# Moving small attention steps behind what they read in an attention-then-SwiGLU kernel

## The chip, the cores and the metric

One core of a Trainium2 chip runs the whole program. The engines are TensorE (PE in the profile; its weight loads are PEld), VectorE (DVE), ScalarE (ACT), GpSimd (POOL) and SyncE (SP), which issues the transfers. Each takes its instructions in program order. The metric is the device time of one execution, in microseconds (us); lower is better.

## The reference

For each of B = 4 batches, x has N = 12416 rows of C = 128 numbers, and 32 inducing points attend to x; then x attends to the result h; then every row goes through a gated unit of width 1536.

```python
def mab(q, kv):
    s = scale * (q @ kv.transpose(0, 2, 1))
    a = np.exp(s - s.max(-1, keepdims=True))
    a /= a.sum(-1, keepdims=True) + 1e-09
    return a @ kv
h = mab(I, x)             # first softmax, over the 12416 rows
y = mab(x, h)             # second softmax, over the 32 points
g = y @ w_gate            # 128 -> 1536
out = (g / (1 + np.exp(-g)) * (y @ w_val)) @ w_out    # 1536 -> 128
```

## The kernel before

The rows of a batch are cut into 25 column tiles of 480 or 512 rows, and the 1536 hidden columns into NT = 12 tiles of 128. One *slot* is one hidden tile of one column tile, so a batch has 25 x 12 = 300 slots. The second attention's product with h is folded into the up-projection weights, so a slot multiplies the softmax weights (the `stack` tile: high and low halves of the second softmax, transposed) by prepared weights.

In a slot TensorE does two up-projections (gate and value, line 900 in batches 1 to 3, lines 859 and 860 in batch 0), ScalarE applies silu (`gates`, line 910), VectorE multiplies (`values`, line 917), ScalarE rounds the product to its high half (`splits`, line 925), GpSimd forms the low half h_lo (line 927), and some slots later TensorE does three down-projections (`back`, lines 944 to 946) into an output tile, whose twelve slots end with an eviction by VectorE (line 954) and a store issued by SP (line 958). Batches 1 to 3 do two slots at a time, a *pair*, named by its first slot; there gate and value each fill one of three double PSUM banks. Some pairs hand half of their high and low halves to VectorE (`owned`). Finished tiles wait in a list `pend` before `back` takes them; the list is held at 8 tiles, and grows to 14 before a *burst*, a slot with a long exponential, in which TensorE lives off the list.

While batch b runs its slots, the attention of batch b+1 is threaded in. `plan` and `post` write a list of (slot, step); at each slot the loop runs all steps whose slot has come, the current batch's first. A step that needs an output bank carries `acc`, and is held back, with all behind it in its list, while the oldest tile of `pend` is the last or one of the first two (three for `hacc`) of its output group.

The steps that matter here:

- `s1_visit`, `s2_visit`: TensorE forms the scores of several chunks of x (line 366; there are 7 chunks), and VectorE takes each out of its bank (s1: line 401; s2 transposes, line 592). The first chunk of a visit takes a bank of the two-bank output pool; so does a visit of a single chunk.
- `size_a` to `size_d`: powers of two that scale h; `size_c` and `size_d` are four tiny ScalarE instructions (`grow`, line 527).
- `s2_max`, `s2_sub` (line 604, GpSimd), then `exp2` (line 607, ScalarE): the second exponential over the whole batch. Its slot is e2, set by the entry E2 of PA (batch 0's loop) and PB (the loops of batches 1 and 2). Then `proj_rounds` and `proj_spread` make the next batch's weights.
- `post`, for each of the 7 column chunks q of the second softmax: `sum2` (VectorE, lines 297 and 298), `rec2` (reciprocal on VectorE, line 614, and for batches 1 to 3 a scaling on ScalarE, line 616), `norm2` (GpSimd, line 620), `aT` (VectorE transpose, line 624), `a_hi` (VectorE, line 627), `a_lo` (GpSimd, line 640), and `spread` (line 657), four transfers per column tile that build its `stack`; tile 0 takes sixteen. aT, a_hi and a_lo have one buffer each; `stack` has three. Chunk 0 is tile 0, each later chunk four tiles.

The steps of chunks 0 and 1 fall at the end of the batch before (bases 266 and 278), the others at bases 26, 74, 122, 170 and 218.

Of the kernel before, what the change touches and what calls it, by code (L numbers as in the profile page):

```python
# [38 lines left out]
NT = DFF // P  # L39
# [14 lines left out]
NST = 3  # L54
# [50 lines left out]
    62: "sb:84:97:1",  # L105
}

PA = dict(LX=(51, 5), S1=(61, 7), MX=7, E1=15, LN=(27, 4), HA=(3, 3, 3), HB=(9, 6), HC=(8, 4), HD=5, H2=6, E2=5, PR=(0, 3), PQ=2)
PB = dict(LX=(0, 9), S1=(25, 7), MX=6, E1=9, LN=(28, 4), HA=(3, 3, 3), HB=(11, 3), HC=(8, 4), HD=6, H2=5, E2=5, PR=(0, 3), PQ=1)


@with_exitstack
def induced_set_attention_then_swiglu(ctx: ExitStack, tc: tile.TileContext, xt, xn, ind, wgv, wo, out):
# [17 lines left out]
    def two():  # L131
        del spare[:]
        return ps_two.tile([P, 2 * 512], F32, name="gw")
# [123 lines left out]
    class Piece:  # L257
# [23 lines left out]
        def add(self):  # L281
            nc.gpsimd.tensor_add(out=self.w.bitcast(I32), in0=self.t.bitcast(I32), in1=self.lw.bitcast(I32))
# [22 lines left out]
    def attention(b, one, xn0=None, xt0=None):  # L305

        st = Batch()
# [304 lines left out]

        def rec2(q):
            nc.vector.reciprocal(out=st.sm[q][:, :FC[q]], in_=st.sm[q][:, :FC[q]])
            if st.half:
                nc.scalar.activation(out=st.sm[q][:, :FC[q]], in_=st.sm[q][:, :FC[q]], func=AF.Copy, scale=2.0 ** TOP)

# [92 lines left out]
    def post(st, q, eng, base, ready=0):  # L710

        f = st.f
        steps = [(0, lambda: f["sum2"](q)), (1, lambda: f["rec2"](q)), (2, lambda: f["norm2"](q, eng)),
                 (5, lambda: f["aT"](q)), (7, lambda: f["a_hi"](q)), (9, lambda: f["a_lo"](q, eng))]
        tiles = [u for u, (p, j) in enumerate(COLS) if p == q]
        return [(base + d, g) for d, g in steps] + [
            (max(base + 12, ready + NT * (u - NST + 1) + 3), lambda u=u: f["spread"](u)) for u in tiles]

    def plan(st, p):

        f, s = st.f, []

        def add(slot, step, *args):
            def go():
                f[step](*args)


            go.acc = (NT - 1, 0, 1) + (2,) * (step == "hacc") if step in ("s1", "max_b", "hacc", "h_c", "s2", "size_b", "s1_visit", "s2_visit") else ()
            s.append((slot, go))

        def blocks(q):
            return CH0[q], CH0[q] + CH[q]

        last = p["S1"][0] + p["S1"][1] * (NCH - 1)
        v1 = last - 3 * p["S1"][1]
        for q in range(NCH):
            add(p["LX"][0] + p["LX"][1] * q if q < NXT else v1 + 1 + 3 * (q - NXT), "load_xt", q)
            if not st.wide:
                add(v1 if q < NXT else last, "s1", q, q not in (0, NXT))
        if st.wide:  # L740
            add(v1, "s1_visit", 0, 1, 2), add(v1, "s1_visit", 3)
            add(last, "s1_visit", 4, 5, 6)
        mb = last + p["MX"]
        add(last + 2, "max_a"), add(mb, "max_b")
        e1 = mb + p["E1"]
        for q in range(NXN):
            add(e1 - p["LN"][0] + p["LN"][1] * q, "load_xn", q)
            add(e1, "exp1_part", q)
            add(e1, "eT", q)
            add(e1 + p["HA"][q], "hacc", q, (0, NXN - 1))  # L750
        add(e1, "exp1_part", NXN, NCH - 1)
        for q in range(NXN, NCH):
            k = NXN + (q - NXN | 1)
            at = e1 + p["HB"][0] + p["HB"][1] * (k - NXN)
            add(max(at - p["HC"][0] - k + q, e1 + 1 + (p["HB"][0] + p["HB"][1] if q == NCH - 1 else p["HA"][0])), "load_xn", q)
            add(at - p["HC"][1] + 1 - k + q, "eT", q)
            add(at, "hacc", q, (k - 1, k))
        add(at, "h_a")
        add(at + 2, "h_b")
        hn = at + p["HD"]  # L760
        add(hn, "h_c")
        for i, step in enumerate(("size_a", "size_b", "size_c", "size_d")):
            add(hn + (2, 8, 12, 16)[i], step)
        for i, q in enumerate(S2O):
            k = i % NXT
            at = hn + 4 + p["H2"] * (NXT - 1) if i < NXT else hn + p["H2"] * (NCH - 1)
            if not st.wide:
                add(at, "s2", *blocks(q), i not in (0, NXT))
            elif i in (0, NXT):
                add(at, "s2_visit", *S2O[i:i + 3])  # L770
            elif i == 3:
                add(at, "s2_visit", q)
            if i + NXT < NCH:
                add(at + 1, "load_xt", S2O[i + NXT])
            d = 2 if i < NXT else 1
            add(at + 1 + d * k, "s2_max", *blocks(q))
            add(at + 3 + (d + 1) * k, "s2_sub", *blocks(q))
        e2 = at + 4 + p["E2"]
        add(e2, "exp2")
        st.e1, st.bursts = e1, {e1, e2}  # L780
        add(e2 + p["PR"][0], "proj_rounds")
        for i in range(2):
            for k in range(NG * NG):
                add(e2 + p["PR"][i] + 3 + k * p["PQ"], "proj_spread", i, k // NG, k % NG)
        for q in range(NF):
            first = [u for u, (p, j) in enumerate(COLS) if p == q][0]
            s += post(st, q, nc.gpsimd, SLOTS + NT * (first - NST) + 2, SLOTS)
        return sorted(s, key=lambda x: x[0])
# [5 lines left out]
    with tc.tile_pool(name="xt0", bufs=NCH - NXT) as xt0, tc.tile_pool(name="xn0", bufs=NCH - NXN) as xn0:  # L794
        cur = attention(0, one, xn0, xt0)
        f = cur.f
# [16 lines left out]
        def run(token):  # L813
# [17 lines left out]
            at=f["aT"], ah=lambda q, e=0: f["a_hi"](q, (f["same"], nc.scalar.copy)[e]),  # L831
# [53 lines left out]
    def twin(x, u):  # L885

        return x.rearrange("p (k w) -> p k w", k=2)[:, :, :u.n]

    def fronts(st, b, c, t):
        us = []  # L890
        g, v = two(), two()
        for k in range(2):
            u = Tile()
            us.append(u)
            u.q, u.j = COLS[c]
            u.b, u.t, u.st, u.whole = b, t + k, st, False
            u.n = WF if u.q == 0 else 32 * FC[u.q]
        for k, x in enumerate((g, v)):
            for u in us:
                nc.tensor.matmul(out=x[:, 512 * (u.t - t):][:, :u.n], lhsT=st.w[:, wcol(k, u.t)], rhs=st.stack[c][:, :u.n], start=True, stop=True)  # L900
        u.g, u.v, u.us = twin(g, u), twin(v, u), us
        return u
# [70 lines left out]
    pend, wait = [], []  # L973
# [14 lines left out]
    for b in range(B):  # L988
        nxt = attention(b + 1, (one, oneb)[(b + 1) % 2]) if b + 1 < B else None
        if nxt is not None:  # L990
            nxt.steps = plan(nxt, PA if b == 0 else PB)
            if b == 0:
                cur.steps.append((nxt.e1, lambda: run(f"e2:52:{NTB}")))
                for q in range(2, NF):
                    base = NT * (1 + NG * (q - 1) - NST) + 2
                    base = max(base, E0 + 4) if q < 4 else max(base, nxt.e1 + 1)
# [14 lines left out]
        for slot2 in range(NT if b == 0 else 0, SLOTS, size):  # L1011
            c, t = slot2 // NT, slot2 % NT
            slots = range(slot2, slot2 + size)
            burst = any(x in bursts for x in slots)
            if size == 1:
                u = front(cur, b, c, t)
                u.us = [u]
                u.last = False
                u.cast_dve = burst or t in CAST
                gate(u)  # L1020
                value(u)
            else:
                u = fronts(cur, b, c, t)
                u.last = b == B - 1 and slot2 == SLOTS - 2
                u.cast_dve = burst
                u.own = u.last or owned(slot2, burst)
                gates(u)
                values(u)
            if wait:
                parts(wait[0])  # L1030
                pend += wait.pop(0).us
            wait.append(u)
            if burst:
                parts(u)
                pend += wait.pop(0).us
            def steps(slot):
                for a in (cur, nxt):
                    while a is not None and a.steps and a.steps[0][0] <= slot:

                        if pend and pend[0].t in getattr(a.steps[0][1], "acc", ()):  # L1040
                            break
                        if getattr(a.steps[0][1], "acc", ()):
                            quiet["step"] = slot + 8
                        a.steps.pop(0)[1]()

            for slot in slots:
                if size == 1:
                    steps(slot)
                ahead = min(ahead + size / RAMP, top_) if nxt is not None and slot < last_burst else max(ahead - 1 / RAMP, low_)
                if slot in bursts:  # L1050
                    ahead = low_ - (b == 0)
                while len(pend) + sum(len(x.us) for x in wait) > ahead + (slot != slots[-1]):
                    back(pend.pop(0))
                if size == 2:
                    steps(slot)
# [46 lines left out]
```

## Time and profile before

| | |
|---|---|
| median of 3 runs | 1446.11 us (1444.27 to 1446.88) |
| the profiled execution | 1444.72 us, span 1442.9 us |
| batch 1 / 2 / 3, first up-projection | 410.34 / 760.61 / 1112.81 us |
| granted TensorE clock | 1.00 |
| second exponential, one instruction | 2.80 us |

In the rows of the profile, "out<-in" names the program's tiles, "xN" is a count, and a bracket at the end of a timeline row is the engine's idle time before that instruction with what ended it. A list of waits has the total in us, the number and the longest.

### The profile page before, as it was taken

What the parts mean: (1) busy time and instruction counts of PE and PEld (TensorE: products, weight loads), DVE (VectorE), ACT (ScalarE), POOL (GpSimd) and SP (SyncE); (2) the same over time, 40 slices, a digit from 0 to 9 for tenths busy, and PEclk for the clock granted to TensorE, in tenths of its full rate; (3) what the DMA queues carried; (4) which work ended last, traced back from release to release, by engine and by line L of the source; (5) the groups of instructions that cost most, each with busy time, mean ns of one, the idle gap of its engine ahead of it and who ended that gap; (6) DMA issues with size and microseconds to landing.
All of it is one profiled execution on the core that took longest, in us unless ns stands there. A gap on an engine that the chain in (4) does not pass through costs nothing. (4 is left out here: it accounts for less than half of the span.)

```text
span 1442.9 us, 22347 instructions
## 1 busy us (share of the span) xinstructions
PE 1398.7 (97%) x7462; PEld 770.0 (53%) x7462; DVE 1184.9 (82%) x1704; ACT 1213.6 (84%) x1600; POOL 1186.1 (82%) x783
## 2 busy tenths in 40 slices
PE   9999999999999999999999999999999999999998
PEld 6577778788854444344444444344444444444444
DVE  6889988888888777688888877778888888888887
ACT  5888788799897888788989888788888888888887
POOL 1689768889888888888888888888888888888887
PEclk9999999999999999999999999999999999999999
DMA  9234522311132432110103413211111001010010
GB/s 370 69 100 133 181 74 90 114 46 46 32 102 75 158 123 99 37 50 29 31 25 114 160 65 126 98 35 41 32 32 32 30 28 32 30 34 27 27 32 28
DMA packets 50803, 107.75 MB, mean 75 GB/s; under 512 B 12928, under 2 KB 32896, under 8 KB 50688
## 3 DMA queue, kind: packets, MB, share of 16 engines
q1 hardware_dynamic: 50688, 106.33, 21.9%
q8 instruction: 59, 0.97, 0.3%
q14 instruction: 56, 0.46, 0.1%
HBM read 62.87 MB, written 25.43 MB: 61 GB/s over the span
## 5 line engine op out<-in xcount | busy, mean ns | idle before, releaser
L927 POOL TENSOR_TENSOR h_lo<-h,h_hi 128x1024 f16<-128x1024 f32 (+2 forms) x450 | 821.4, 1840 | 154.2 <-ACT h_hi L925 151.2
L917 DVE SCALAR_TENSOR_TENSOR h<-gw,sc,silu 128x1024 f32<-128x1024 f32 (+2 forms) x450 | 502.1, 1117 | 163.8 <-ACT silu L910 151.6
L910 ACT ACTIVATE silu<-gw,sc 128x1024 f32<-128x1024 f32 (+1 forms) x451 | 489.3, 1086 | 99.0 <-PE gw L900 45.4
L925 ACT CAST h_hi<-h 128x1024 f16<-128x1024 f32 (+3 forms) x446 | 404.3, 907 | 14.0 <-DVE h L917 13.4
L944 PE MATMUL o<-h_hi,work 128*128 128x512 f16 (+1 forms) x900 | 335.8, 373 | 0.3 <-DVE h_lo L927 0.3
L945 PE MATMUL o<-h_hi,work 128*128 128x512 f16 (+1 forms) x900 | 335.8, 373 | 0.0
L946 PE MATMUL o<-h_lo,work 128*128 128x512 f16 (+1 forms) x900 | 335.8, 373 | 0.0
L900 PE MATMUL gw<-stack,work 128*128 128x512 f16 (+1 forms) x1200 | 303.6, 373 | 18.1 <-ACT silu L910 16.5
L883 POOL TENSOR_TENSOR h_lo<-h,h_hi 128x512 fp32r<-128x512 f32 (+1 forms) x216 | 269.5, 1272 | 56.4 <-ACT h_hi L881 35.0
L900 PEld LDWEIGHTS <-work 128*128 128x128 f16 x1200 | 116.4, 98 | 158.1 <-issue 29.5
L865 ACT ACTIVATE silu<-gv 128x512 f32<-128x512 f32 (+1 forms) x300 | 176.6, 590 | 25.8 <-PE gv L859 20.3
L873 DVE TENSOR_TENSOR h<-gv,silu 128x512 f32<-128x512 f32 (+1 forms) x216 | 143.4, 667 | 35.5 <-ACT silu L865 16.5
L900 PE MATMUL gw<-stack,tw 128*128 128x512 f16 (+1 forms) x600 | 152.4, 373 | 10.6 <-ACT silu L910 9.6
L944 PEld LDWEIGHTS <-work 128*128 128x128 f16 x900 | 88.1, 98 | 102.7 <-issue 2.9
L945 PEld LDWEIGHTS <-work 128*128 128x128 f16 x900 | 87.8, 98 | 101.9 <-issue 3.7
L946 PEld LDWEIGHTS <-work 128*128 128x128 f16 x900 | 87.9, 98 | 100.6
L881 ACT CAST h_hi<-h 128x512 fp32r<-128x512 f32 (+1 forms) x190 | 115.4, 607 | 10.2 <-DVE h L873 8.6
L859 PE MATMUL gv<-stack,tw 128*128 128x512 f32 (+1 forms) x300 | 120.2, 401 | 2.9 <-DVE stack L701 1.2
L860 PE MATMUL gv<-stack,tw 128*128 128x512 f32 (+1 forms) x300 | 116.8, 389 | 0.7 <-ACT silu L865 0.4
L944 PE MATMUL o<-h_hi,wo_lo 128*128 128x512 f32 (+1 forms) x288 | 112.6, 391 | 0.0
L946 PE MATMUL o<-h_lo,wo_hi 128*128 128x512 f32 (+1 forms) x288 | 111.3, 387 | 0.1
L945 PE MATMUL o<-h_hi,wo_hi 128*128 128x512 f32 (+1 forms) x288 | 111.0, 385 | 0.0
(217 smaller groups left out, 1373.8 us busy)
## 6 DMA issues: line engine op xcount, KB each, us to landing
xt_sb<-xt SPq DMA_DIRECT2D x32, 896.0 KB, 5.1
xn_sb<-xn SPq DMA_DIRECT2D x18, 896.0 KB, 6.5
out<-ob SPq DMA_DIRECT2D x52, 256.0 KB, 2.0
out<-ob SPq DMA_DIRECT2D x48, 240.0 KB, 2.0
xt_sb<-xt SPq DMA_DIRECT2D x4, 832.0 KB, 4.7
xn_sb<-xn SPq DMA_DIRECT2D x3, 832.0 KB, 4.6
stack<-a_hi SPq DMA_DIRECT2D x72, 32.0 KB, 1.8
stack<-a_lo SPq DMA_DIRECT2D x72, 32.0 KB, 1.8
```

Source lines behind the costliest of these rows:

```text
L859: nc.tensor.matmul(out=u.g[:, :n], lhsT=st.w[:, wcol(0, t)], rhs=rhs, start=True, stop=True)
L865: nc.scalar.activation(out=u.s[:, :u.n], in_=u.g[:, :u.n], func=AF.Silu)
L873: nc.vector.tensor_mul(out=u.h[:, :n], in0=u.v[:, :n], in1=u.s[:, :n])
L883: eng.tensor_sub(out=u.lo[:, :n], in0=u.h[:, :n], in1=u.hi[:, :n].bitcast(F32))
L900: nc.tensor.matmul(out=x[:, 512 * (u.t - t):][:, :u.n], lhsT=st.w[:, wcol(k, u.t)], rhs=st.stack[c][:, :u.n], start=True, stop=True)
L910: nc.scalar.activation(out=f(u.s), in_=f(u.g), func=AF.Silu, scale=u.st.g)
L917: nc.vector.scalar_tensor_tensor(out=h, in0=f(u.v), scalar=u.st.k, in1=f(u.s), op0=ALU.mult, op1=ALU.mult)
L925: (nc.vector.tensor_copy if h is u.x else one_wide if u.cast_dve else nc.scalar.copy)(out=f(u.hi), in_=h)
L927: (nc.vector if h is u.x else nc.gpsimd).tensor_sub(out=f(u.lo), in0=h, in1=f(u.hi))
L944: nc.tensor.matmul(out=o[:, :n], lhsT=w_lo[:, ws], rhs=u.hi[:, :n], start=(t == 0), stop=False)
L945: nc.tensor.matmul(out=o[:, :n], lhsT=w_hi[:, ws], rhs=u.hi[:, :n], start=False, stop=False)
L946: nc.tensor.matmul(out=o[:, :n], lhsT=w_hi[:, ws], rhs=u.lo[:, :n], start=False, stop=(t == NT - 1))
```

## The change

`rec2` is split: the ScalarE scaling becomes a step of its own, `scale2`. For batches 1 to 3 it comes five slots after the reciprocal, and the steps behind it come 5 (norm2), 6 (aT, a_hi, a_lo, and the first spread's own offset) slots later than before. The second exponential moves from E2 = 5 to 8 in batch 0's loop and to 11 in those of batches 1 and 2, and with it the burst and the weights behind it. The single-chunk visits come two slots after the visits of three. `size_c` and `size_d` come 8 and 10 slots later. At the first pair of batch 1, where the PSUM pools change, one finished tile's `back` is issued ahead of the first up-projections.

```diff
-PA = dict(..., E2=5, PR=(0, 3), PQ=2)
-PB = dict(..., E2=5, PR=(0, 3), PQ=1)
+PA = dict(..., E2=8, PR=(0, 3), PQ=2)
+PB = dict(..., E2=11, PR=(0, 3), PQ=1)
...
         def rec2(q):
             nc.vector.reciprocal(out=st.sm[q][:, :FC[q]], in_=st.sm[q][:, :FC[q]])
+
+        def scale2(q):
             if st.half:
                 nc.scalar.activation(out=st.sm[q][:, :FC[q]], in_=st.sm[q][:, :FC[q]], func=AF.Copy, scale=2.0 ** TOP)
...
-        steps = [(0, lambda: f["sum2"](q)), (1, lambda: f["rec2"](q)), (2, lambda: f["norm2"](q, eng)),
-                 (5, lambda: f["aT"](q)), (7, lambda: f["a_hi"](q)), (9, lambda: f["a_lo"](q, eng))]
+        at = (1, 6, 7, 11, 13, 15, 18) if st.half else (1, 2, 2, 5, 7, 9, 12)
+        steps = [(0, lambda: f["sum2"](q)), (at[0], lambda: f["rec2"](q)), (at[1], lambda: f["scale2"](q)), (at[2], lambda: f["norm2"](q, eng)),
+                 (at[3], lambda: f["aT"](q)), (at[4], lambda: f["a_hi"](q)), (at[5], lambda: f["a_lo"](q, eng))]
...
-            (max(base + 12, ready + NT * (u - NST + 1) + 3), lambda u=u: f["spread"](u)) for u in tiles]
+            (max(base + at[6], ready + NT * (u - NST + 1) + 3), lambda u=u: f["spread"](u)) for u in tiles]
...
-            add(v1, "s1_visit", 0, 1, 2), add(v1, "s1_visit", 3)
+            add(v1, "s1_visit", 0, 1, 2), add(v1 + 2, "s1_visit", 3)
...
-            add(hn + (2, 8, 12, 16)[i], step)
+            add(hn + (2, 8, 20, 26)[i], step)
...
             elif i == 3:
-                add(at, "s2_visit", q)
+                add(at + 2, "s2_visit", q)
...
+                if b == 1 and slot2 == 0:
+                    back(pend.pop(0))
                 u = fronts(cur, b, c, t)
```

More of the change, by code (lines that the diff above doesn't have):

```diff
@@ L106 @@
 }
-PA = dict(LX=(51, 5), S1=(61, 7), MX=7, E1=15, LN=(27, 4), HA=(3, 3, 3), HB=(9, 6), HC=(8, 4), HD=5, H2=6, E2=5, PR=(0, 3), PQ=2)
-PB = dict(LX=(0, 9), S1=(25, 7), MX=6, E1=9, LN=(28, 4), HA=(3, 3, 3), HB=(11, 3), HC=(8, 4), HD=6, H2=5, E2=5, PR=(0, 3), PQ=1)
+PA = dict(LX=(51, 5), S1=(61, 7), MX=7, E1=15, LN=(27, 4), HA=(3, 3, 3), HB=(9, 6), HC=(8, 4), HD=5, H2=6, E2=8, PR=(0, 3), PQ=2)
+PB = dict(LX=(0, 9), S1=(25, 7), MX=6, E1=9, LN=(28, 4), HA=(3, 3, 3), HB=(11, 3), HC=(8, 4), HD=6, H2=5, E2=11, PR=(0, 3), PQ=1)
 @with_exitstack
```

## The prediction

> **What bounds the kernel now.** I read the page first, then the list of waits for TensorE, then the same list for the engines that TensorE waits for, then the timeline at single places.
>
> ```profile
> span 1442.9 us, 22347 instructions
> PE 1398.7 (97%) x7462; PEld 770.0 (53%) x7462; DVE 1184.9 (82%) x1704; ACT 1213.6 (84%) x1600; POOL 1186.1 (82%) x783
> ```
>
> TensorE is the bound, so only its stalls are worth anything. The list of waits of TensorE (who waited for whom, total us, times, longest), and the same row in the windows 410 to 438 and 760 to 790 us, where batches 1 and 2 begin; and, from TensorE's timeline, its stall behind the second exponential of batch 1's loop:
>
> ```profile
> PE gw L900 <- ACT silu L910: 26.1, 27, 1.9
> PE o L366 <- DVE s_all L592: 2.1, 2, 1.1
> ```
> ```profile
> PE gw L900 <- ACT silu L910: 1.1, 4, 0.5
> PE gw L900 <- ACT silu L910: 0.9, 2, 0.7
> ```
> ```profile
> 602.59 0.59 PE L900 MATMUL gw<-stack,work 128*128 128x512 f16 x2 [1.94 <-ACT silu L910]
> ```
>
> The up-projections of batches 1 to 3 wait 26.1 us for ScalarE's silu: the silu that frees their PSUM bank is late. What makes ScalarE late is in ScalarE's own list:
>
> ```profile
> ACT sm L616 <- DVE sm L614: 34.3, 19, 2.1
> ...
> ACT s_all L607 <- POOL s_all L604: 6.4, 2, 3.2
> ACT sm L616 <- DVE negmax L419: 3.1, 2, 1.6
> ```
>
> Line 616 is the scaling of the second softmax's reciprocals, issued right behind VectorE's reciprocal of line 614. ScalarE waits there 21 times (19 + 2), two of them in batch 0's loop, 19 in batches 1 to 3; and twice, 3.2 us each, the second exponential (L607) waits for GpSimd's subtractions.
>
> One such place in batch 3 (slots 172 to 176). ScalarE, then VectorE, then TensorE by pairs of slots (each window runs from one pair's first up-projection to the next; length, busy time, matmuls):
>
> ```profile
> 1301.17 0.98 ACT L925 CAST h_hi<-h 128x960 f16<-128x960 f32 x1
> 1304.17 0.21 ACT L616 ACTIVATE sm<-sm 128x15 f32<-128x15 f32 x1 [2.02 <-DVE sm L614]
> 1304.29 1.04 ACT L910 ACTIVATE silu<-gw,sc 128x960 f32<-128x960 f32 x1
> ```
> ```profile
> 1302.99 0.65 DVE L297 TENSOR_REDUCE pairs<-s_all 128x15 f32<-128x480 f32 x1
> 1303.67 0.18 DVE L298 TENSOR_REDUCE sm<-pairs 128x15 f32<-128x30 f32 x1
> 1303.89 0.25 DVE L614 RECIPROCAL sm<-sm 128x15 f32<-128x15 f32 x1
> 1305.43 1.22 DVE L917 SCALAR_TENSOR_TENSOR h<-gw,sc,silu 128x960 f32<-128x960 f32 x1 [1.29 <-ACT silu L910]
> ```
> ```profile
> 1301.58:1303.60 2.02, 2.02 (x11) 1.00 0.00 0
> 1303.60:1307.00 3.40, 2.19 (x11) 1.00 0.00 0
> 1307.00:1309.15 2.15, 2.15 (x11) 1.00 0.00 0
> ```
>
> The reader should see a chain: VectorE is a pair behind, ScalarE stands 2.02 us for a 0.21 us instruction, the silu behind it starts late, and a pair takes 3.40 us in place of 2.02, the next 2.15. The loss is 1.38 + 0.13 = 1.51 us, while TensorE's idle time there is 3.40 - 2.19 = 1.21: 0.30 more. The granted clock is 1.00 in all three, so no part of it is the clock.
>
> The Trainium skill (Perfetto Trace Analysis, Identifying the Most-Contended Engine) warns that matmul busy time says little about headroom, since matmuls are pipelined; the trace agrees by these 0.30 us. By idle time alone the next sum would be 20.2 where start-to-start lengths give 25.9.
>
> **The change, part by part.** The sum is made against the profiled execution, 1444.72 us (span 1442.9); the median of the runs is 1446.11, 1.4 above.
>
> *1. scale2 five slots behind rec2 (b > 0), its followers moved along.* No instruction is added. Of the 26.1 us, 2.0 belong to the batch starts and 3.9 to the two second exponentials (part 3), so 20.2 us in 27 - 6 - 2 = 19 stalls are left, one for each ScalarE wait in batches 1 to 3. With 0.30 more each: 20.2 + 5.7 = 25.9 us. In the new order ScalarE reaches scale2 three pairs, some 6 us, behind VectorE's reciprocal, so the wait goes. What is late next is VectorE, which keeps its work: free at 1304.1, it does pair 172's products by 1305.3 and, for a pair half handed to it, cast and subtraction (about 0.65 each, as the reduction of the same 480 columns), and starts pair 174's products near 1306.6, 3.0 us behind that pair's first matmul. How late they may be:
>
> ```profile
> 1310.16 1.18 DVE L917 SCALAR_TENSOR_TENSOR h<-gw,sc,silu 128x960 f32<-128x960 f32 x1
> ```
> ```profile
> 1311.19 0.37 PE L900 MATMUL gw<-stack,work 128*128 128x480 f16 x1
> ```
>
> Pair 176 (first matmul 1307.00) had its products at 1310.16, 3.15 us behind, and pair 180, which needs that bank, began at 1311.19, 2.04 behind its predecessor: no stall. So 3.0 just fits. I leave 0.1 us per place (bounds 0 and 1.0, the latter if VectorE stays late): 25.9 - 1.9 = 24.0 us.
>
> The followers (norm2 on GpSimd, aT and a_hi on VectorE, a_lo on GpSimd, first spread on SP) come 4 to 6 slots later. For one chunk this puts aT and a_hi behind the first exponential's burst, not ahead of it. VectorE stands idle there once:
>
> ```profile
> 514.89 1.28 DVE L917 SCALAR_TENSOR_TENSOR h<-gw,sc,silu 128x1024 f32<-128x1024 f32 x1 [3.42 <-ACT silu L910]
> ```
>
> aT comes behind these products in program order and misses that gap; the two operations (0.65 us each) delay products by at most one of them. I take 0.3 us in each of two batches (bounds 0 and 0.65): -0.6.
>
> The spreads are SP's. Tile 0's sixteen transfers (slot 279, now 284) fall behind the output store of tile 23, which they preceded; SP takes its queue in order and that store waits for VectorE:
>
> ```profile
> SPq L958 <- DVE ob L954: 592.9, 71, 14.1
> ```
> ```profile
> 734.52 2.41 SPq L657 DMA_DIRECT2D stack<-a_hi  x4
> 737.91 2.41 SPq L657 DMA_DIRECT2D stack<-a_lo  x4
> 740.36 2.49 SPq L657 DMA_DIRECT2D stack<-a_hi  x4
> 742.89 2.49 SPq L657 DMA_DIRECT2D stack<-a_lo  x4
> 746.70 0.34 SPq L958 DMA_DIRECT2D out<-ob  x1
> ```
> ```profile
> 748.31 0.67 DVE L627 TENSOR_REDUCE a_hi<-aT 128x512 f16<-128x512 f32 x1
> ```
> ```profile
> DMA to landing us min/median/max: 1.7/1.8/8.0
> ```
>
> There is one a_hi buffer: the a_hi of chunk 1 (748.31) must wait until the twelfth transfer (last of the second a_hi group) has landed. Before, that was about 742.9 + 1.2 = 744.1, 4 us early. Now the sixteen start at 747.1; the twelfth is issued 11 x 0.62 us later, at 753.9, and lands at 755.7. The a_hi comes six slots later, 748.31 + 6.06 = 754.4: VectorE waits 1.3 us. With its own lateness (up to 0.9) against the 1.1 us it may be late, that stalls TensorE 0 to 1.2 us, and chunk 1's a_lo on GpSimd waits likewise for the sixteenth, with the h_lo of later tiles queued behind it; TensorE has eight tiles in store against that. I take 0.7 at two boundaries and 0.3 at the first, where slots are issued singly: -1.7 (bounds 0 and -6). The Trainium skill (DMA: Bandwidth & Descriptors, Anatomy of one DMA) gives about 2.0 us as the fixed part, for GpSimd's path; by it each landing is 0.2 later than by the row's 1.8 and the sum 0.6 us smaller.
>
> In batch 0's loop both scale waits go as well. TensorE's one idle row near them:
>
> ```profile
> 392.64 0.48 PE L859 MATMUL gv<-stack,tw 128*128 128x480 f32 x1 [1.00 <-DVE h L873]
> ```
>
> VectorE also does other work there, so I take 0.8 (bounds 0 and 1.0).
>
> *2. Fourth chunk of scores two slots on.* In the first softmax no wait of TensorE stands at this chunk, so 0; the code also holds that step back while the oldest stored tile is the last or one of the first two of an output group, so it comes at slot 51. In the second the wait is the row of 2.1 us, twice 1.07:
>
> ```profile
> 567.31 0.91 PE L366 MATMUL o<-xt_sb,hTs 128*32 128x416 f32 x8 [1.07 <-DVE s_all L592]
> ```
>
> Its 0.91 us of matmuls stay, now behind the next pair, when VectorE has emptied the bank: +2.1 (bounds 1.5 and 2.3). That pair also gets scale2 and size_c's three scalings, four ScalarE instructions of about 0.21; the chunk's 0.91 us cover them.
>
> *3. Second exponential six slots on (three in batch 0).* ScalarE and GpSimd in batch 1:
>
> ```profile
> 592.84 1.28 ACT L607 ACT_TABLE_LOAD   x1
> 597.31 2.80 ACT L607 ACTIVATE s_all<-s_all 128x3104 f32<-128x3104 f32 x1 [3.19 <-POOL s_all L604]
> 600.13 1.28 ACT L910 ACT_TABLE_LOAD   x1
> ```
> ```profile
> 596.34 0.94 POOL L604 TENSOR_TENSOR s_all<-s_all,mx2b 128x448 f32<-128x448 f32 x1
> ```
>
> ScalarE does no silu for 8.57 us, 3.19 of it waiting; TensorE's stored work covers all but the 1.94 us shown first. Without the wait 5.4 us are left, under the 6.6 that were covered. GpSimd's last subtraction ends at 597.28, plus about 1 us for the norm2 that now joins its queue; the exponential, ready at 594.1, comes six slots (6.4 us) later, less some 2.5 us that are saved ahead of it (a stall of 1.4 as above, 1.1 at the chunk), at 598.0: 0.3 us of wait at worst. Gain 2 x (1.94 + 0.30) = 4.5, less 0.3: 4.2 (bounds 2.0 and 4.5). If GpSimd's h_lo are late after it, tiles stored fewer: -0.5 (0 to -2). Batch 0's exponential has no wait row: 0.
>
> *4. size_c and size_d later:* ScalarE's list has no wait at their line, so 0. *5. One down-projection ahead of batch 1's first up-projection:* it fills up to 0.65 us of waiting, but that up-projection starts no sooner and the pairs behind it wait for silu anyway (1.1 us in the window from 410): 0 (bounds 0 and 0.65).
>
> Sum: 24.0 - 0.6 - 1.7 + 0.8 + 2.1 + 4.2 - 0.5 = 28.3 us. 1444.7 - 28.3 = 1416.4; on the median's footing 1446.1 - 28.3 = 1417.8.
>
> **The rivals.**
>
> *VectorE takes ScalarE's place.* For: 3.0 us of lateness against 3.15 is thin, and the stall that went also gave VectorE time to catch up. Against: the delay of aT and a_hi takes two operations out of those very pairs. With 0.8 us left at each of 19 places: 19 x 0.7 = 13.3 less gain, 1431.
>
> *SP's sixteen transfers cost more.* For: six slots of distance shrink to nothing. Against: the eight stored tiles. With 2 us more at three boundaries: 1424.
>
> *Everything is covered.* No residue and none of the new costs: 25.9 + 0.8 + 2.1 + 4.5 = 33.3 us, 1412.8; with the rest of the bounds 1411.
>
> *Nothing gained:* ScalarE's waits are replaced one for one. Against it, 6 us lie between reciprocal and scaling where 2.02 were missing. 1446.
>
> *Slower.* Tile 0 of the next batch isn't there when its batch begins, at this row:
>
> ```profile
> 760.61 0.38 PE L900 MATMUL gw<-stack,tw 128*128 128x512 f16 x1
> ```
>
> On the clock of this trace, with the sixteen set behind the store, the last lands at 747.1 + 15 x 0.62 + 1.8 = 758.2, so 2.4 us remain. It decides from 2.4 + 28.3/3 = 11.8 us of extra delay at each of three boundaries; with 14 us each the time is 1446 + 6 = 1452. Nothing in the rows is near that.
>
> **How the numbers follow.** Forecast 0.60, VectorE 0.14, SP 0.11, all covered 0.08, nothing gained 0.04, slower 0.03. The forecast's own range is 1412 to 1424; the whole range 1410 to 1431 takes in the all-covered, the SP and most of the VectorE case and leaves out some 0.15. A measurement of this kernel tells 0.2% (2.9 us) from no change. Faster 0.93, same 0.04, slower 0.03; I say 1417.5 us.
>
> **What would show it.** ScalarE's list without the rows L616 and L607; TensorE's row L900 from silu down from 26.1 to a few us; no wait of L366 on line 592; pairs of 2.0 to 2.2 us at slots 174 and 222. A row of a_hi (L627) on VectorE waiting for a DMA, at slot 290, would show the SP cost. A large row of L900 waiting for VectorE's line 917 would make the prediction wrong by the first rival.

## The result and the profile after

The changed kernel takes 1419.53 us (median of 6; 1418.42 to 1420.85) beside 1446.23 us before (6 runs): a ratio of 0.9817, 95% interval 0.9805 to 0.983, 26.7 us less. The profiled execution took 1419.16 us.

The page of the changed kernel (its lines lie 2 to 3 further down than before: up-projections 903, silu 913, products 920, h_lo 930, down-projections 947 to 949, a_hi 629, a_lo 642, stores 961):

```profile
span 1417.4 us, 22310 instructions
...
PE 1396.9 (99%) x7462; PEld 771.9 (54%) x7462; DVE 1185.2 (84%) x1704; ACT 1215.3 (86%) x1600; POOL 1184.7 (84%) x783
```

TensorE's busy time is 1.8 us less than before and the span 25.5 us: what went is idle time. Its list of waits:

```profile
PE gw L903 <- DVE h L920: 3.5, 4, 1.8
PE gw L903 <- ACT silu L913: 2.2, 7, 0.7
PE o L947 <- DVE h_lo L930: 2.1, 4, 0.7
```

The 26.1 us for silu are 2.2, and the row of the fourth chunk (L366 on line 592) is gone. The two rows that wait for VectorE were there before, and have grown:

```profile
PE gw L900 <- DVE h L917: 0.9, 2, 0.4
PE o L944 <- DVE h_lo L927: 0.3, 1, 0.3
```

ScalarE at the place that the prediction followed, slot 176 of batch 3, and TensorE by pairs there (slots 172, 174, 176):

```profile
1285.50 0.21 ACT L618 ACTIVATE sm<-sm 128x15 f32<-128x15 f32 x1
```
```profile
1278.55:1280.58 2.03, 2.03 (x11) 1.00 0.00 0
1280.58:1282.60 2.02, 2.02 (x11) 1.00 0.00 0
1282.60:1284.70 2.10, 2.10 (x11) 1.00 0.00 0
```

The scaling has no bracket: it waited for nothing. The pair that took 3.40 us takes 2.02, the next 2.10.

The second exponential in batch 1's loop, on ScalarE:

```profile
593.47 1.28 ACT L607 ACT_TABLE_LOAD   x1
594.77 2.79 ACT L607 ACTIVATE s_all<-s_all 128x3104 f32<-128x3104 f32 x1
598.98 1.28 ACT L913 ACT_TABLE_LOAD   x1 [1.42 <-PE gw L903]
```

It starts right behind its table, and ScalarE now waits for TensorE behind it.

Where the growth comes from is seen at the end of batch 1, on SyncE, VectorE, GpSimd and TensorE, with the pair of slot 296 in a window of its own at the end (length, busy time, matmuls):

```profile
734.59 0.34 SPq L961 DMA_DIRECT2D out<-ob  x1
735.02 2.41 SPq L659 DMA_DIRECT2D stack<-a_hi  x4
737.53 2.43 SPq L659 DMA_DIRECT2D stack<-a_lo  x4
740.01 2.49 SPq L659 DMA_DIRECT2D stack<-a_hi  x4
742.54 2.49 SPq L659 DMA_DIRECT2D stack<-a_lo  x4
```
```profile
743.74 0.69 DVE L629 TENSOR_REDUCE a_hi<-aT 128x512 f16<-128x512 f32 x1 [1.40 <-DMA stack<-a_hi]
746.15 0.66 DVE L930 TENSOR_TENSOR h_lo<-o,h_hi 128x480 f16<-128x480 f32 x1
```
```profile
746.40 1.16 POOL L642 TENSOR_TENSOR a_lo<-aT,a_hi 128x512 f16<-128x512 f32 x1 [2.28 <-DMA stack<-a_lo]
```
```profile
745.60 0.56 PE L903 MATMUL gw<-stack,work 128*128 128x480 f16 x2 [0.83 <-DVE h L920]
746.86 0.36 PE L947 MATMUL o<-h_hi,work 128*128 128x480 f16 x1 [0.69 <-DVE h_lo L930]
```
```profile
744.20:748.06 3.86, 2.34 (x11) 1.00 0.04 6
```

Tile 0's sixteen transfers follow the store of tile 23. Chunk 1's a_hi waits 1.40 us for the second a_hi group to land, VectorE's products and its own h_lo halves come late behind it, and the pair is 1.84 us too long. TensorE waits for VectorE's h_lo not as an operand: in a pair that shares its halves with VectorE, `values` puts half of the product into a bank of the output pool (tile o in the row of 746.15), and the down-projections at slot 296 are those of slot 288, the first of an output tile, which take a bank of that pool (746.86, right behind the end of h_lo at 746.81). The tiles in store are no help against this wait.

By stages, from the starts of up-projections in the timelines (us; batch 3 to the end of the span; p1_only and no_p1 are experiments below):

| stage | before | after | p1_only | no_p1 |
|---|---|---|---|---|
| batch 0, slot 283 to its end | 21.11 | 20.71 | 20.72 | 21.15 |
| batch 1, slots 0 to 28 | 26.81 | 26.15 | 26.82 | 26.16 |
| batch 1, 28 to 124 | 120.92 | 118.28 | 118.14 | 121.28 |
| batches 1 / 2, 124 to 132 (fourth chunk) | 14.39 / 14.38 | 12.07 / 12.08 | 11.83 / 11.83 | 12.87 / 12.87 |
| batches 1 / 2, 132 to 160 (exponential) | 40.37 / 40.36 | 38.60 / 38.60 | 43.11 / 41.18 | 38.60 / 38.60 |
| batches 1 / 2, 160 to 284 | 131.19 / 131.19 | 126.30 / 126.30 | 126.31 / 126.31 | 131.19 / 131.20 |
| batches 1 / 2, 284 to the next batch | 16.58 / 16.57 | 18.56 / 19.53 | 18.56 / 18.78 | 16.58 / 16.58 |
| batch 2, 0 to 124 | 149.69 | 146.95 | 146.92 | 151.98 |
| batch 3 | 330.14 | 323.85 | 323.96 | 330.01 |

### The profile page after: what moved, and what is told of

Its sections match the earlier page's. It is cut to its first block, busy times and chain, and to the rows that moved or that the text cites. A ratio compares the mean times of both kernels' runs of the same rounds, so it can differ in the third digit from the quotient of the medians.

```text
span 1417.4 us, 22310 instructions
## 1 busy us (share of the span) xinstructions
PE 1396.9 (99%) x7462; PEld 771.9 (54%) x7462; DVE 1185.2 (84%) x1704; ACT 1215.3 (86%) x1600; POOL 1184.7 (84%) x783
## 4 chain that ended last, share of the span: by engine, by line
PE 79%; DVE 8%; ACT 7%; issue 3%; POOL 1%; DMA 1%; SPq 1%; DVEq 0%; ACTq 0%; POOLq 0%
PE gw L903 20%; PE o L947 14%; PE o L949 14%; PE o L948 14%; PE gv L863 4%; PE gv L862 4%; DVE h L920 4%; ACT silu L913 3%; ACT h_hi L928 1%; PE gv L366 1%; DVE h_hi L928 1%; PE o L439 1%; PE o L366 1%; PE gw L366 1%; SPq L659 1%
```

## The experiments

Theory: ScalarE standing in its queue behind VectorE's reciprocal cost most, and the later spreads give part of it back at the ends of batches. Rivals: the gains need each other; VectorE takes ScalarE's place; five slots are needed.

**p1_only**: the kernel before with the split of rec2 and the offsets `at`, nothing else.

> Only the split of rec2 and the later followers; exponential, fourth chunk, size steps and the extra down-projection as before. My theory (the scale waits were the bulk, the boundaries give some back): the 19 silu stalls of about 1.4 us go, VectorE's a_hi of chunk 1 waits for the sixteen transfers at two boundaries, the waits of 1.07 us at L366 and 1.94 us behind the second exponential stay: 1446.2 - 20 = 1426, between 1423 and 1429. Rival (the parts hide each other's stalls): the gain is much less than the changed kernel's 26.7 less the 6.5 of the other parts, 1432 or more.

1427.19 us, ratio 0.9871 (0.9858 to 0.9885): 18.9 us where 20 were expected, inside the range. Two expectations failed. The fourth chunk's wait is gone here too, though it is in its old place. TensorE's rows of the first and the fourth chunk (both in tile o; before, the fourth waited until VectorE had emptied the first's bank), and VectorE's transposition of the first:

```profile
559.45 0.96 PE L366 MATMUL o<-xt_sb,hTs 128*32 128x448 f32 x8
...
561.73 0.88 PE L366 MATMUL o<-xt_sb,hTs 128*32 128x416 f32 x8
```
```profile
560.58 0.64 DVE L592 STREAM_TRANSPOSE s_all<-o 128x448 f32<-128x448 f32 x1
```

The bank is empty at 561.2, before the fourth chunk wants it: that wait was VectorE's lateness at the same place. The exponential, on the other hand, waits longer: in batch 1 ScalarE has its table 5.6 us sooner than before, and GpSimd's last subtraction starts only 4.5 us sooner (591.87 against 596.34). TensorE's stall behind it grows from 1.94 to 3.0 us. ScalarE's row:

```profile
592.83 2.79 ACT L607 ACTIVATE s_all<-s_all 128x3104 f32<-128x3104 f32 x1 [4.31 <-POOL s_all L604]
```

**no_p1**: the changed kernel with the old offsets, scale2 in rec2's slot.

```diff
-        at = (1, 6, 7, 11, 13, 15, 18) if st.half else ...
+        at = (1, 1, 2, 5, 7, 9, 12) if st.half else ...
```

> All of the change but the split: scale2 in the slot of rec2 and the followers at their old slots. My theory: the 19 scale waits come back with their silu stalls, no a_hi waits for a transfer, and the exponential and the fourth chunk give 2.1 + 4.2 = 6.3 us: 1440, between 1438 and 1442. Rival (parts hide each other): under 3 us or over 9 us.

1438.04 us, 0.9954 (0.9941 to 0.9966): 8.1 us, at the upper edge. TensorE's first row and ScalarE's:

```profile
PE gw L903 <- ACT silu L913: 21.6, 27, 1.5
```
```profile
ACT sm L618 <- DVE sm L614: 34.4, 19, 2.1
```

The scale waits are all there. 18.9 + 8.1 = 27.0 against 26.7 for both: the totals add, though inside them part of the fourth chunk's gain comes with either (14.39 to 12.87 without part 1, to 11.83 with part 1 alone) and the exponential's is larger once part 1 is in (38.60 against 43.11 and 41.18 in the table).

**p3_only**: the kernel before with E2 = 8 and 11.

> Only E2 = 8 and 11. My theory: ScalarE's wait of 3.2 us for GpSimd at L607 goes in both batches, and with it the stall of 1.94 us and the 0.3 behind it: 4.2 us, 1442. Rival: the exponential's own 5.4 us of silence is what stalls TensorE, so the time stays within 1 us of 1446.2.

1441.68 us, 0.9975 (0.9966 to 0.9984): 4.5 us, where the theory said 4.2; in its trace slots 132 to 160 take 38.60 us in both batches, 3.5 us less than before, as in the changed kernel. The row L607 is gone from ScalarE's list; TensorE's silu row is 23.0.

**spread_early**: the changed kernel with tile 0's transfers ahead of the store.

```diff
-            (max(base + at[6], ...
+            (max(base + (16 if st.half and q == 0 else at[6]), ...
```

> The changed kernel with tile 0's sixteen transfers at slot 282 and so ahead of tile 23's output store in SyncE's queue, 284 and behind it before; nothing else. My theory (the store in the queue makes a_hi's one buffer late): the transfers start near 730.4 in place of 735.0, the twelfth lands some 3 us before a_hi of chunk 1, VectorE's and GpSimd's waits for DMA (3.8 and 5.5 us) go, and the pairs at slot 296 lose 1.86 + 2.83 us less: 1415, between 1413.5 and 1416. Rival (VectorE and GpSimd are full at that place anyway): the DMA waits go and the time stays within 1 us of 1419.5.

1415.69 us, 0.9793 (0.978 to 0.9806): 3.8 us below the changed kernel's 1419.53. From slot 284 to the next batch it takes 17.06 and 17.00 us. SyncE and the a_hi that waited:

```profile
730.67 2.42 SPq L659 DMA_DIRECT2D stack<-a_hi  x4
...
738.20 2.49 SPq L659 DMA_DIRECT2D stack<-a_lo  x4
740.78 6.89 SPq L961 DMA_DIRECT2D out<-ob  x2
```
```profile
742.51 0.67 DVE L629 TENSOR_REDUCE a_hi<-aT 128x512 f16<-128x512 f32 x1
```

Two slots in a list moved the transfers by more than 4 us, since they no longer stand behind a store that waits for VectorE.

**own_buffers**: the changed kernel, chunk 0's a_hi and a_lo in buffers of their own.

```diff
-            st.ah[q] = sgl.tile([P, WF], F32R, name="a_hi")
+            st.ah[q] = sgl.tile([P, 64], F32R, name="a_hi0") if st.half and q == 0 else sgl.tile([P, WF], F32R, name="a_hi")
...
-            st.al[q] = sgl.tile([P, WF], F32R, name="a_lo")
+            st.al[q] = sgl.tile([P, 64], F32R, name="a_lo0") if st.half and q == 0 else sgl.tile([P, WF], F32R, name="a_lo")
```

> The changed kernel with buffers of their own for chunk 0's a_hi and a_lo (128 columns each), so that chunk 1's a_hi and a_lo wait for no transfer; SyncE's order stays as in the changed kernel, store first. My theory (the one buffer is what carries the lateness of the transfers to VectorE and GpSimd): the waits of 3.8 and 5.5 us go although the transfers still start late, and the time is that of spread_early, 1415.7, between 1414.5 and 1417. Rival (the late transfers hurt elsewhere, at the next batch's first tile or through SyncE's queue): part of the 4 us stays, or TensorE waits at slot 0: 1418 or more.

1414.70 us, 0.9786 (0.9771 to 0.98); 16.87 and 16.82 us from slot 284 to the next batch. The transfers are as late as in the changed kernel, a_hi doesn't wait:

```profile
734.86 2.41 SPq L659 DMA_DIRECT2D stack<-a_hi  x4
```
```profile
742.10 0.67 DVE L629 TENSOR_REDUCE a_hi<-aT 128x512 f16<-128x512 f32 x1
```

So the store in the queue makes the transfers late, and the single buffer is what hands that to VectorE and GpSimd; undoing either gives most of the loss back (16.58 us before).

**visits_back**: spread_early without part 2 (both single-chunk visits at their old slots).

> spread_early with both single-chunk visits back at the slots of the visits of three, so without part 2. Theory (the wait of 1.07 us at the fourth chunk was VectorE's lateness behind the scale wait, and part 1 alone removes it; p1_only has no such row): nothing is lost, and two pairs in each of two batches are some 0.24 us shorter: 1414.7, between 1413.5 and 1416. Rival (the bank has to be emptied first, whatever else runs): the wait comes back, 1417.5 or more.

1414.26 us, 0.9783 (0.9769 to 0.9798), 1.4 us less than spread_early in another set of runs. In its trace slots 124 to 132 take 11.83 us in place of 12.08, and 38 to 80 take 51.16 in place of 51.40, in batch 2 alike. Part 2 costs some 0.24 us at four places once part 1 is in.

**near**: the changed kernel with nearer offsets.

```diff
-        at = (1, 6, 7, 11, 13, 15, 18) if st.half else ...
+        at = (1, 4, 5, 8, 10, 12, 15) if st.half else ...
```

> The changed kernel with the scaling three slots behind the reciprocal in place of five, and norm2, aT, a_hi, a_lo and the first spread at 5, 8, 10, 12 and 15 in place of 7, 11, 13, 15 and 18. Theory: 2.02 us were missing and two pairs are 4 us, so no scale wait comes back; tile 0's transfers come at slot 281, ahead of the store, so the boundary losses go; VectorE has aT and a_hi nearer to the reciprocal, up to 0.2 us at each of 19 places: 1417, between 1414.5 and 1419.5. Rival (five slots are needed): rows L616 come back in ScalarE's list and the time is 1422 or more.

1413.89 us, 0.9779 (0.9764 to 0.9794), below the range of 1414.5 to 1419.5 that was expected. No scaling waits for VectorE, so five slots are not needed. VectorE's lateness was expected to cost up to 0.2 us at each place; slots 160 to 284 take 125.86 us, 0.44 less than in the changed kernel. There the pairs of slots 188 and 236, whose down-projections open an output tile, take 2.24 and 2.25 us, and here 2.02: the farther offsets were the costlier ones. The boundaries of batches 1 and 2 are at 16.44 us, but batch 0's, where slots come singly, now has the wait (21.21 us from slot 283 to its end):

```profile
400.77 0.69 DVE L629 TENSOR_REDUCE a_hi<-aT 128x512 f16<-128x512 f32 x1 [1.42 <-DMA stack<-a_hi]
```

**dve_scale**: the kernel before, the scaling on VectorE, no step moved.

```diff
-                nc.scalar.activation(out=st.sm[q][:, :FC[q]], in_=st.sm[q][:, :FC[q]], func=AF.Copy, scale=2.0 ** TOP)
+                nc.vector.tensor_scalar(out=st.sm[q][:, :FC[q]], in0=st.sm[q][:, :FC[q]], scalar1=2.0 ** TOP, scalar2=None, op0=ALU.mult)
```

> The kernel before with the scaling of line 616 done by VectorE in its old slot; no step is moved. Theory (ScalarE standing in its queue is the cause, not where the steps are): the row L616 and the 19 silu stalls go, tile 0's transfers stay early, the second exponential's wait stays or grows as in p1_only; VectorE gets 0.2 us more at each place with aT and a_hi close behind, and I expect up to 0.4 us of stall left at each of 19: 1430, between 1424 and 1434. Rival (VectorE takes ScalarE's place): the stalls of TensorE name VectorE's line 917 and the time is 1440 or more.

1425.46 us, 0.9853 (0.9837 to 0.987): 20.1 us without moving a step, inside the range. TensorE's and ScalarE's rows:

```profile
PE gw L900 <- ACT silu L910: 6.4, 9, 2.2
PE o L944 <- DVE h_lo L927: 1.9, 8, 0.4
PE gw L900 <- DVE h L917: 1.4, 4, 0.4
```
```profile
ACT s_all L607 <- POOL s_all L604: 6.6, 2, 3.5
```

The cause is ScalarE standing in its queue, not where the steps lie. VectorE shows up with 1.9 and 1.4 us (0.3 and 0.9 before), far from the rival's 1440: slots 160 to 284 take 126.68 us and batch 3 324.26, some 0.1 us more at each place than in the changed kernel.

**together**: near, own_buffers and visits_back in one kernel.

> The nearer offsets of near, the buffers of own_buffers and the visits of visits_back in one kernel; second exponential, size steps and extra down-projection as in the changed kernel. Theory (three separate causes): from near's 1413.9 the visits give 1.0 back and the wait for the transfers at the start of batch 1, which near alone shows (1.4 us on VectorE), gives 1.0 to 1.3: 1411.7, between 1410.5 and 1413.5. Rival (the nearer offsets and the buffers repair the same loss): 1413 to 1414.

1411.41 us, 0.9758 (0.9744 to 0.9772): the best version, 8.1 us below the changed kernel. Batch 0 takes 19.71 us from slot 283 to its end, less than in any other run (21.11 before, 20.71 in the changed kernel, 21.21 in near), and no a_hi waits for a transfer.

**no_back**: the changed kernel without the extra down-projection.

> The changed kernel without the one down-projection ahead of batch 1's first up-projection. My prediction's view (the pairs behind wait for silu anyway): within 0.2 us of 1419.5. Rival (the 0.65 us of waiting are filled with work that has to be done in any case, and the later pairs have room): 0.65 us longer, 1420.2, all of it in slots 0 to 28 of batch 1.

1421.19 us, 0.9826 (0.981 to 0.9841); the intervals overlap with the changed kernel's, but its trace has 26.82 us in slots 0 to 28 of batch 1, as before, where the changed kernel has 26.15, and no other stage of the table differs by more than 0.2 (its profiled execution also opens 1.4 us later; see the last section). The rival holds: the 0.65 us are gained. ScalarE at the second pair of batch 1, in no_back and in the changed kernel:

```profile
414.40 1.12 ACT L913 ACTIVATE silu<-gw,sc 128x1024 f32<-128x1024 f32 x1 [1.08 <-PE gw L903]
```
```profile
412.30 1.11 ACT L913 ACTIVATE silu<-gw,sc 128x1024 f32<-128x1024 f32 x1 [0.41 <-PE gw L903]
```

## Why the prediction was right, point by point

1417.5 us was said, 1419.53 came. Part for part, against the table:

- *The scale waits.* 24.0 us were said for 19 places; without the two at slot 126 that is 21.4. The stages that hold the other 17 (28 to 124 and 160 to 284 of batch 1, 0 to 124 and 160 to 284 of batch 2, batch 3) lost 2.64 + 4.89 + 2.74 + 4.89 + 6.29 = 21.45. That the two agree so closely is in part luck: these stages also hold the load of the last section, for which TensorE waited 1.5 us before and 0.9 after, and part 2's 0.24 us in each of two batches, and the two nearly cancel. Start-to-start lengths, not idle time, were the right measure, and VectorE's 3.0 us against 3.15 did fit. The first rival is out: TensorE's row for VectorE's products did grow to 3.5 us, but 2.6 of them are the waits of 0.8 and 1.8 us at the two boundaries, and dve_scale, which gives VectorE the scaling as well, lost only some 0.1 us more per place.
- *The fourth chunk.* With the stall beside it 4.7 us were said and 4.62 came, but the step "in the second the wait is the row of 2.1 us, so +2.1" named the wrong cause: part 1 alone takes that wait away, and the move itself costs 0.24 us per place.
- *The second exponential.* 4.2 - 0.5 = 3.7 us said, 1.77 + 1.76 = 3.5 measured. That ScalarE would come 2.5 us earlier and make a larger wait without the move shows in p1_only (4.31 us).
- *SP's sixteen transfers.* The mechanism came as written: the store first, a_hi waiting, 1.3 us said, 1.40 and 2.42 measured at the two boundaries (at the second SP took 3.35 us for the first four transfers in place of 2.41; why, the runs don't show). The term was mis-sized: 0.7 us each said, and the stage behind slot 284 grew by 1.98 and 2.96, of which the transfers account for 1.50 and 2.53 (what spread_early gives back). The step that failed is the one from VectorE's wait to TensorE's: it counted on eight stored tiles, and left out that VectorE's h_lo halves hold a bank of the output pool, for which the down-projections that open an output tile wait (0.69 us behind the 0.83 for the products; 0.36 also at slot 284, which stays in spread_early). The 0.3 at batch 0's boundary did not come.
- *Batch 0's scale waits* gave 0.4, not 0.8. *aT and a_hi behind the first exponential* (-0.6) left no mark. *The extra down-projection* was put at 0 and gave 0.65: ScalarE itself waits for the up-projections there (1.08 us at the second pair in no_back, 0.41 in the changed kernel), so the silus moved forward with them.

The sum of the measured parts is 21.45 + 4.62 + 3.53 + 0.40 + 0.66 - 4.94 = 25.7 us, where 28.3 was said. The boundary term alone is 3.2 us off; the others add up to 0.7 us the other way, and that the loss of 0.6 which did not come and the gain of 0.65 which was not counted make up for part of it is luck.

The Trainium skill (Perfetto Trace Analysis, Identifying the Most-Contended Engine) warns that matmul busy time is no good measure of the room that is left, since pipelined matmuls look smaller in the trace. The runs agree: without the 0.30 us beyond idle time at each of the 17 places, 5.1 us would have been missing from the 21.4.

## What to carry to other kernels

A tiny instruction that reads what another engine has just been handed costs the whole distance between the two queues, and every instruction behind it pays. Give it little more than the distance that the wait row shows: here the wait was 2 us, two pairs (4 us) were enough, and three pairs with the later followers cost more; one pair was not tried. When steps move, write down which ones change order in a transfer queue and which single buffers their data sit in: here that one swap cost some 4 of 31 us, and one small buffer got them back. And look which banks an engine that comes late still holds: work in store is no help when the next piece needs such a bank.

## What the runs showed that was not expected

The load of the last x chunk in batch 2's loop is late by an amount that differs between the profiled executions at the same place. The longest of TensorE's waits there (all batches, L439 waiting for xn_sb) is 0.7 us in dve_scale, 0.9 in the changed kernel and 3.0 in p3_only; the rows of dve_scale and p3_only:

```profile
PE o L439 <- DMA xn_sb<-xn: 1.0, 2, 0.7
```
```profile
PE o L439 <- DMA xn_sb<-xn: 3.3, 2, 3.0
```

The kernel's opening differs too: batch 0's first up-projection on line 859 (862 after the change) starts at 37.27 us before, 37.47 in the changed kernel, 38.91 in no_back and 38.96 in no_p1, though no edit touches what stands ahead of it. A profiled execution can thus stand over 3 us above its kernel's median (p3_only: 1444.96 against 1441.68; no_p1: 1441.75 against 1438.04), which is as much as the smaller parts here are worth; their sizes were therefore read stage by stage. Each kernel has one profiled execution, so what makes these two places vary is not shown.
